# The first three rows of w4's last piece load ahead of the other w4 pieces, in transfers of 125 and of 3 partitions

## The chip, the core and the metric

The kernel runs on one core of a Trainium2 chip. A core has the engines PE (matrix multiply, with its weight loads PEld), DVE, ACT, POOL and SP, and sixteen DMA engines that move data between HBM and the on-chip memory SBUF, which has 128 partitions. Every load of this kernel but one is issued from SP. The metric is the device time of one execution in microseconds (us): the median of three runs is 218.01 (217.16 to 218.03).

## The reference

Two branches are computed for four tokens (B = 4, D = 576) and added to the input; all tensors are bf16.

- A: the token is normalized and multiplied by wq into 32 query heads of 128. Each pair of query heads attends to the last 2048 positions of one of 16 key/value heads; the result goes through wo (4096 x 576).
- B: an MLP. With one token per sequence its first shifted part adds zero, so that the branch is x plus gelu(layernorm(x) @ w3) @ w4, with w3 of 576 x 4608 and w4 of 4608 x 576.

```
xn = layernorm(x)
q = xn @ wq ;  p = softmax(q k^T * Dh^-0.5) ;  A = (p v) @ wo
h2 = gelu(layernorm(x1) @ w3) @ w4 ;  B = x1 + h2        # x1 = xn here
out = x + A + B
```

The keys and values that are read are 2 x 16 heads x 4 sequences x 2048 positions x 128 x 2 bytes, 67 MB; the weights bring the reads to 87.17 MB.

## The kernel before, in words

All large loads go through SP's queue in the order in which the program issues them. First come wq's five pieces and the 16 K tiles of 2 MB, one for each key/value head (`kv_load`, L98 to L102), with w3's five pieces between the first of them; then w4's first nine rows, then the 16 V tiles of 2 MB with the eight pieces of wo between them (L427 to L440), and last the remaining 27 row groups of w4.

A "row" of w4 in this text is one row group: `w4_src` (L106) views w4 as `[e, m, i, n]` with e = 2 halves, m = 128 partitions, i = 18 rows and n = 576 columns. One row holds 128 x 576 numbers, that is 1,152 bytes on each partition (144 KB). `load_w4(e, i0, n, cuts)` (L396 to L405) takes one buffer of the pool `w` (three buffers, used in turn) for n rows and issues one transfer for each entry of `cuts`. `mlp_out(t, e, i0, n)` (L407 to L409) multiplies: two matmuls of 288 columns for each row, which accumulate into the PSUM tile ACC (`acc_matmuls`, L328 to L331).

The end of the program is written out by hand:

```
    end = load_w4(0, 9, 9, (9,)) + load_w4(1, 0, 9, (9,)) + load_w4(1, 9, 9, (4, 2, 2, 1))   # L444
    run_later()
    mlp_out(*end[0])
    while later:
        run_later()
    for part in end[1:]:
        mlp_out(*part)
```

So six transfers follow the last V tile on SP: nine rows, nine rows, then the last piece of nine in cuts of four, two, two and one. PE takes them in the order of the list `end`: nine rows of the first, then what the list `later` still holds (the projection of the last head pair through wo, `project`, four rows of wo with two matmuls each), then nine, four, two, two and one rows. After the last matmul DVE copies ACC to the tile `fin` (L455), and SP and ACT each write half of the output with a transfer of 4 partitions (L457).

Each transfer from SP adds to one of eight semaphores, used in turn, and SP issues a transfer only after the transfer before it on the same semaphore has landed in full; so at most eight transfers are under way. A transfer of 128 partitions is shared by all sixteen DMA engines, each of which takes its share of every transfer in the order of issue and closes it with a 4-byte packet that adds one to the semaphore; the transfer has landed when the last engine has closed it.

Of the kernel before, what the change touches and what calls it, by code (L numbers as in the profile page):

```python
# [11 lines left out]
BF16 = mybir.dt.bfloat16  # L12
# [9 lines left out]
def kernel(  # L22
# [18 lines left out]
    nc = tc.nc  # L41
    P = 128
    B, Sq, D = A_x.shape
# [44 lines left out]
    wpl = ctx.enter_context(tc.tile_pool(name="w", bufs=NWP))  # L88
# [17 lines left out]
    w4_src = B_w4.rearrange("(e m i) n -> e m i n", e=2, i=NFH)  # L106
# [119 lines left out]
    for y in range(NY):  # L226
        tq = ps_o.tile([P, 2 * HB, P], BF16, tag="O", name=f"tq{y}")
        for k in range(2):
            for m in range(HB):
                nc.tensor.transpose(out=tq[:, k * HB + m, :],  # L230
                                    in_=q_rows[:, k, m, y, :, :].rearrange("p g i -> p (g i)"), identity=ident[:])
# [110 lines left out]
    def head_out(h):  # L342


        O, T = O_tiles.pop(h)
        on = small.tile([P, rep, B], BF16, tag="on")
        nc.vector.tensor_copy(out=on[:].rearrange("p r b -> p b r"), in_=O)  # L347

        def select():
            for x in range(XR):  # L350
                nc.tensor.matmul(out=T[0:32, x, :], lhsT=ident[:, x:P:XR], rhs=on[:].rearrange("p r b -> p (r b)"),  # L351
                                 start=(x == 0), stop=(x == XR - 1), skip_group_check=True)
            g2, odd = divmod(h, 2)
            if not odd:
                onx_tiles[g2] = small.tile([P, XR, B], BF16, tag="onx", name=f"onx{g2}")
            onx = onx_tiles[g2]
            for r in range(rep):
                q = 32 * (2 * odd + r)
                nc.vector.tensor_copy(out=onx[q:q + 32, :, :], in_=T[0:32, :, r * B:(r + 1) * B])  # L359
            if odd:  # L360
                wt = wo_tiles.pop(g2)
                onx_tiles.pop(g2)

                def project():
                    for x in range(XR):
                        acc_matmuls(onx[:, x, :], lambda a, z, x=x: wt[:, x, a:z])
                later.append(project)
        later.append(select)

    def run_later():  # L370
        fns = later[:]
        later.clear()
        for fn in fns:
            fn()
# [21 lines left out]
    def load_w4(e, i0, n, cuts):  # L396
        t = wpl.tile([P, n, D], BF16, tag="w", name=f"w4_{e}_{i0}")
        parts = []
        a = 0
        for m in cuts:  # L400
            nc.sync.dma_start(out=t[:, a:a + m, :], in_=w4_src[e, :, i0 + a:i0 + a + m, :])
            parts.append((t[:, a:a + m, :], e, i0 + a, m))
            a += m
        assert a == n
        return parts  # L405
# [29 lines left out]
    for v in range(Hkv):  # L435
# [5 lines left out]
        run_later()  # L441
        v_compute(v)
        head_out(v)
    end = load_w4(0, 9, 9, (9,)) + load_w4(1, 0, 9, (9,)) + load_w4(1, 9, 9, (4, 2, 2, 1))  # L444
    run_later()
    mlp_out(*end[0])
    while later:
# [40 lines left out]
```

## Time and profile before

| what | value |
|---|---|
| median of three runs | 218.01 us (217.16, 218.01, 218.03) |
| the profiled execution's own time | 217.48 us |
| its span | 215.6 us (1.9 us lie around it) |
| bytes read from HBM | 87.17 MB, 404 GB/s over the span |
| PE busy, DVE busy, ACT busy | 115.0, 108.9, 21.1 us |
| mean granted PE clock | 0.675 |
| share of the last chain: DMA, DVE, PE, ACT | 70%, 13%, 8%, 5% |

How to read it: times are in us from the span's start. The page's second part cuts the span into 40 equal slices of 5.39 us; a digit is a share in tenths. The windows view gives for chosen stretches the busy time of each engine, the granted PE clock (1.00 is full speed), the mean busy share of the sixteen DMA engines and the GB/s moved. The timeline lists instructions in order of time with start and duration. The trace also records every DMA packet (start, duration, bytes, queue, but not the DMA engine's number) and the moment of each addition to a semaphore.

### The profile page before, as it was taken

The numbers are of one execution on the slowest core, as the hardware profiler recorded it, in microseconds if no ns is written. First come the engines' busy times: TensorE is split into PE (matmuls) and PEld (weight loads), VectorE is DVE, ScalarE is ACT, GpSimd is POOL, SyncE is SP. The second block draws the span as 40 slices with busy tenths as digits, with TensorE's granted clock in tenths as the row PEclk, the third lists the DMA queues.
The fourth block names the chain that finished last, engine by engine and source line by source line (L and its number), as shares of the span: only waits on it lengthen the run. The fifth ranks groups of instructions, "written<-read, shape, count | busy, mean of one in ns | idle before, by whom it ended". The sixth has DMA issues, their size and how long they took to land.

```text
span 215.6 us, 5534 instructions
## 1 busy us (share of the span) xinstructions
PE 115.0 (53%) x2577; PEld 74.3 (34%) x2577; DVE 108.9 (51%) x156; ACT 21.1 (10%) x36; POOL 1.8 (1%) x8
## 2 busy tenths in 40 slices
PE   0343788748644554445424098748662634536383
PEld 0110744426311111111101087747452434434341
DVE  7932967584999999989785592201100000001000
ACT  0202220000000000000003896100000000000000
POOL 1110000000000000000000000000000000000000
PEclk9999999658767667558588557555555555555559
DMA  6999999999999999999999999999999999999970
GB/s 259 432 418 442 413 436 433 405 439 407 433 426 432 417 423 429 426 429 432 410 438 417 435 411 428 428 417 389 417 430 420 418 433 420 429 422 423 422 288 18
DMA packets 8255, 87.52 MB, mean 406 GB/s; under 512 B 925, under 2 KB 1065, under 8 KB 2729
## 3 DMA queue, kind: packets, MB, share of 16 engines
q1 hardware_dynamic: 8216, 87.17, 96.1%
q8 instruction: 20, 0.33, 0.6%
q14 instruction: 3, 0.02, 0.0%
q10 hardware_dynamic: 16, 0.01, 0.0%
HBM read 87.17 MB, written 0.00 MB: 404 GB/s over the span
## 4 chain that ended last, share of the span: by engine, by line
DMA 70%; DVE 13%; PE 8%; ACT 5%; issue 2%; SPq 1%; DVEq 0%; ACTq 0%
DMA t<-in_A_k_cache_dram 36%; DMA t<-in_A_v_cache_dram 21%; DMA w<-in_B_w_dram 9%; DVE kt L258 6%; DMA wq<-in_A_wq_dram 3%; PE pt L306 3%; PE O L325 2%; ACT E L283 2%; DVE qz L177 2%; PE qp L204 1%; ACT PZ L312 1%; ACT pr L300 1%; DVE mx L279 1%; DVE pr L302 1%; PE ACC L330 1%
## 5 line engine op out<-in xcount | busy, mean ns | idle before, releaser
L258 DVE STREAM_TRANSPOSE kt<-t 128x2048 int32<-128x2048 int32 x32 | 72.3, 2292 | 12.8 <-DMA t<-in_A_k_cache_dram 12.8
L267 PE MATMUL S<-kt,qz 32*32 32x512 bf16 x1024 | 36.9, 625 | 38.0 <-DVE kt L258 36.6
L325 PE MATMUL O<-PZ,t 128*128 128x8 bf16 x1024 | 30.3, 168 | 26.2 <-DMA t<-in_A_v_cache_dram 22.6
L325 PEld LDWEIGHTS <-t 128*128 128x128 bf16 x1024 | 29.0, 104 | 30.2 <-DMA t<-in_A_v_cache_dram 25.2
L347 DVE CAST on<-O 128x8 bf16<-128x8 f32 x16 | 2.7, 167 | 57.9 <-PE O L325 57.8
L267 PEld LDWEIGHTS <-qz 32*32 32x32 bf16 x1024 | 10.8, 94 | 60.6 <-issue 57.4
L306 PE MATMUL pt<-ident,pr 128*128 128x128 bf16 x64 | 6.7, 292 | 9.4 <-DVE pr L302 8.2
L383 PEld LDWEIGHTS <-w 128*128 128x128 bf16 x144 | 9.2, 162 | 5.2 <-DMA w<-in_B_w_dram 2.7
L383 PE MATMUL ACC<-ln2T,w 128*128 128x4 bf16 x144 | 9.6, 202 | 1.7 <-DMA w<-in_B_w_dram 1.7
L330 PE MATMUL ACC<-wo,onx 128*4 128x288 bf16 x64 | 9.0, 436 | 2.2 <-DVE onx L359 2.2
L283 ACT ACTIVATE E<-S,nb 128x512 f32<-128x512 f32 x4 | 4.0, 1115 | 59.5 <-DVE nb L281 59.5
L306 PEld LDWEIGHTS <-pr 128*128 128x128 bf16 x64 | 5.9, 135 | 10.0 <-ACT pr L300 10.0
L300 ACT ACTIVATE pr<-E,rdm 128x512 bf16<-128x512 f32 x6 | 8.1, 1430 | 0.8 <-DVE rdm L289 0.8
L359 DVE CAST onx<-O 32x16 bf16<-32x16 f32 x32 | 5.3, 165 | 5.3 <-PE O L351 4.9
L330 PE MATMUL ACC<-w,gT 128*4 128x288 bf16 x72 | 7.5, 368 | 0.8 <-DMA w<-in_B_w_dram 0.7
L302 DVE TENSOR_SCALAR pr<-E,rdm 128x512 bf16<-128x512 f32 x10 | 6.5, 809 | 0.3 <-PE pt L306 0.2
L204 PE MATMUL qp<-wq,xnT 128*4 128x512 bf16 x32 | 4.0, 620 | 4.5 <-DMA wq<-in_A_wq_dram 4.5
L224 DVE CAST q_rows<-qp 128x256 bf16<-128x256 f32 x8 | 2.9, 410 | 6.4 <-PE qp L204 6.4
L351 PE MATMUL O<-on,ident 128*32 128x8 bf16 x64 | 4.1, 171 | 3.6 <-DVE on L347 3.6
L351 PEld LDWEIGHTS <-ident 128*32 128x32 bf16 x64 | 4.4, 110 | 3.4 <-issue 3.1
L330 PEld LDWEIGHTS <-gT 128*4 128x4 bf16 x72 | 3.9, 104 | 4.7 <-issue 2.1
L330 PEld LDWEIGHTS <-onx 128*4 128x4 bf16 x64 | 3.7, 110 | 4.3 <-DVE onx L359 2.6
(67 smaller groups left out, 51.0 us busy)
## 6 DMA issues: line engine op xcount, KB each, us to landing
t<-in_A_k_cache_dram SPq DMA_DIRECT2D x16, 2048.0 KB, 24.7
t<-in_A_v_cache_dram SPq DMA_DIRECT2D x16, 2048.0 KB, 29.3
w<-in_B_w_dram SPq DMA_DIRECT2D x4, 1152.0 KB, 13.3
wo<-in_A_wo_dram SPq DMA_DIRECT2D x8, 576.0 KB, 21.3
wq<-in_A_wq_dram SPq DMA_DIRECT2D x4, 1024.0 KB, 6.3
w<-in_B_w_dram SPq DMA_DIRECT2D x3, 1296.0 KB, 30.3
w_t<-in_B_w_dram SPq DMA_DIRECT2D x1, 576.0 KB, 14.4
w<-in_B_w_dram SPq DMA_DIRECT2D x1, 576.0 KB, 25.1
```

What stands on the lines that cost most here:

```text
L204: nc.tensor.matmul(out=qp[k][32 * i:32 * i + B, :], lhsT=lhsT, rhs=rhs, start=False, stop=False, skip_group_check=True)
L258: nc.vector.transpose(out=ap32(kt, e * G * 2, [[2 * G * 2, NCH // 2], [1, 2], [2, G]]), in_=ap32(kn, e * G, [[2 * 2 * G, NCH // 2], [2 * G ...
L267: nc.tensor.matmul(out=S[g][32 * b:32 * b + 32, :].rearrange("p (c k l) -> p c k l", k=GK, l=2), lhsT=qz[32 * g:32 * g + 32, b, h, y, :], ...
L283: nc.scalar.activation(out=E[:, :, g, :].rearrange("p (c l) k -> p c k l", l=2), in_=S[g][:].rearrange("p (c k l) -> p c k l", k=GK, l=2), ...
L300: nc.scalar.mul(out=dst, in_=src, mul=rdm[:, b:b + 1])
L302: nc.vector.tensor_scalar_mul(out=dst, in0=src, scalar1=rdm[:, b:b + 1])
L306: nc.tensor.transpose(out=tp[:, cc, :], in_=pr[:, half * HC + cc, :, :, :].rearrange("p g k b -> p (g k b)"), identity=ident[:])
L325: nc.tensor.matmul(out=O, lhsT=vn[:, c, :], rhs=PZ[:, c, :].rearrange("p (b n) -> p b n", b=B)[:, :, h * rep:(h + 1) * rep], start=(c == 0 ...
L330: nc.tensor.matmul(out=ACC[32 * q:32 * q + B, 0:DH], lhsT=lhsT, rhs=rhs_cols(q * DH, (q + 1) * DH), start=False, stop=False, skip_group_ch ...
L351: nc.tensor.matmul(out=T[0:32, x, :], lhsT=ident[:, x:P:XR], rhs=on[:].rearrange("p r b -> p (r b)"), start=(x == 0), stop=(x == XR - 1), ...
L359: nc.vector.tensor_copy(out=onx[q:q + 32, :, :], in_=T[0:32, :, r * B:(r + 1) * B])
L383: nc.tensor.matmul(out=gp[:, fc, :], lhsT=lhsT, rhs=rhs, start=False, stop=False, skip_group_check=True)
```

## The change

Only the end changes. The tile of the last piece, `end_t`, is taken from the pool first. Its rows 0 to 2 are loaded right behind the last V tile, in one transfer of partitions 0 to 124 and one of partitions 125 to 127. Then come the two pieces of nine rows as before, and then the six remaining rows of the last piece in cuts of three, two and one. In PE's order the three rows stand behind the first nine rows and the projection, and ahead of the second nine. Seven transfers take the place of six; bytes, matmuls and what is computed stay the same.

```
-    end = load_w4(0, 9, 9, (9,)) + load_w4(1, 0, 9, (9,)) + load_w4(1, 9, 9, (4, 2, 2, 1))
+
+    end_t = wpl.tile([P, 9, D], BF16, tag="w", name="w4_end")
+    for p0, p1 in ((0, 125), (125, P)):
+        nc.sync.dma_start(out=end_t[p0:p1, 0:3, :], in_=w4_src[1, p0:p1, 9:12, :])
+    end = load_w4(0, 9, 9, (9,)) + [(end_t[:, 0:3, :], 1, 9, 3)] + load_w4(1, 0, 9, (9,))
+    for a, m in ((3, 3), (6, 2), (8, 1)):
+        nc.sync.dma_start(out=end_t[:, a:a + m, :], in_=w4_src[1, :, 9 + a:9 + a + m, :])
+        end.append((end_t[:, a:a + m, :], 1, 9 + a, m))
     run_later()
     mlp_out(*end[0])
     while later:
```

## The prediction

> **What bounds the kernel now.** I read the page's slices first, then the queues, then the chain of waits from 140 us on, then the windows of the last 10 us, and last PE's timeline there.
>
> ```profile
> PEclk9999999658767667558588557555555555555559
> DMA  6999999999999999999999999999999999999970
> GB/s 259 432 418 442 413 436 433 405 439 407 433 426 432 417 423 429 426 429 432 410 438 417 435 411 428 428 417 389 417 430 420 418 433 420 429 422 423 422 288 18
> ```
>
> The DMA engines are full in every slice from the second to the 38th. So the loads set the pace, and only the two ends of the span can be shortened without moving fewer bytes. The slice from 204.8 to 210.2 us moves 288 GB/s in place of some 422.
>
> ```profile
> 161.02 30.25 DMA t<-in_A_v_cache_dram
> ...
> 191.29 20.30 DMA w<-in_B_w_dram
> ...
> 211.63 0.68 PE ACC L330 x6
> ...
> 212.33 0.45 DVE fin L455
> ```
>
> The chain ends with the V tiles, w4's last transfers, six matmuls and the copy of ACC. After the copy stand the output's transfers, up to 215.6, which the change leaves alone.
>
> ```profile
> 204.00:206.00 2.00, 1.04 (x24) 0.83 (x23) 0.50 (x3) 0.00 (x0) 0.00 (x0) 0.50 1.00 417
> 206.00:208.00 2.00, 2.00 (x21) 1.07 (x17) 0.00 (x0) 0.00 (x0) 0.00 (x0) 0.50 0.88 344
> 208.00:209.00 1.00, 1.00 (x12) 0.53 (x10) 0.00 (x0) 0.00 (x0) 0.00 (x0) 0.50 0.53 209
> 209.00:210.00 1.00, 1.00 (x12) 0.57 (x10) 0.00 (x0) 0.00 (x0) 0.00 (x0) 0.50 0.42 150
> 210.00:211.00 1.00, 1.00 (x18) 0.64 (x16) 0.00 (x0) 0.00 (x0) 0.00 (x0) 0.83 0.26 83
> 211.00:212.00 1.00, 0.89 (x14) 0.41 (x9) 0.00 (x0) 0.00 (x0) 0.00 (x0) 1.00 0.07 23
> ```
>
> The last three columns are granted clock, DMA share and GB/s. The share falls in steps from 206 to 212: the sixteen engines do not finish together. Idle engine time there is 0.24 + 0.47 + 0.58 + 0.74 + 0.93 = 2.96 us for each engine on average; that is the most a perfect spread could take from the last landing. The additions to the semaphores say who is late: in the one-row transfer six engines close from 207.92 to 208.07, two at 208.26 and 208.85, four from 210.04 to 210.27, four from 211.46 to 211.96. The same groups stand in the last V tile (first 198.37, last 202.50).
>
> ```profile
> q1 hardware_dynamic: 8216, 87.17, 96.1%
> q8 instruction: 20, 0.33, 0.6%
> ...
> q10 hardware_dynamic: 16, 0.01, 0.0%
> ```
>
> Why they are late is in queue q8: 20 packets of 16 KB of instructions. Chaining the packet records (the next packet of an engine starts 3 or 4 ns before the last one ends) puts nearly all of them on eight engines in a fixed rotation, so that four have had three and four have had two; each costs its engine about 1.4 us. The other eight lead.
>
> The same windows show the second limit: PE is full from 206 to 211, at half clock until 210.33.
>
> ```profile
> 205.64 2.32 PE L330 MATMUL ACC<-w,gT 128*4 128x288 bf16 x18 [0.70 <-DMA w<-in_B_w_dram]
> 207.75 1.17 PE L330 MATMUL ACC<-wo,onx 128*4 128x288 bf16 x8
> 208.75 3.54 PE L330 MATMUL ACC<-w,gT 128*4 128x288 bf16 x36
> ```
>
> From the landing of the first nine rows (205.60) to the end PE works off 62 matmuls, 31 rows. Starts of successive rows lie 0.24 us apart at half clock and 0.12 at full clock. The second nine land at 208.70, just as PE is free; PE then waits only for the last two pieces (landed 211.58 and 211.96), about 0.3 us in all. So the last landing binds, but PE is only 0.4 us behind it.
>
> **The change, part by part.**
>
> *How the transfer is shared out.* Queue q1 counts 8216 packets: 57 transfers of 128 partitions with 128 + 16 closing packets make 8208, and one output transfer of 4 partitions with 4 + 4 makes the other 8; q10's 16 are two of 4 partitions. So 128 partitions run on 16 engines and 4 on four, evenly in both rows. The largest even split of 125 in at most 16 is five engines with 25 partitions each, of 3 on three. No transfer here shows 125: the bounds are one engine and sixteen. On one engine the 432 KB take 16.7 us at the price below, its first nine rows land at 201.5 + 16.7 = 218.2 and the end comes 12.6 us later, 230; I give that under 1 in 100. I take five, since both rows split evenly over as many as divide them. [...]
>
> *Price of the move.* A row of 3,456 bytes lies between those of 2,304 (eight take 0.735 us on an engine, 25.1 KB/us) and of 4,608 (1.40 us, 26.3 KB/us); I use 25.8. Each of the five gets 25 x 3.456 = 86.4 KB, 3.35 us, ahead of the second-to-last pieces, and three of them 0.13 more. In return every engine has 27.6 KB, 1.07 us, less behind the second nine. Net: eleven engines end 1.07 earlier, five end 2.28 later (2.41 with the small transfer).
>
> *One more transfer on SP.* An issue takes 0.33 us. The waits of SP for its eight semaphores come up once more; the last issue now waits for wo's last piece (landed 197.6) rather than V's tile before last (196.2), 8 us before any engine is through the last V tile and its w4 rows. Nothing queues behind it but the output. Price zero; if that lead were gone, the 1.4 us between the two landings. The tile takes an earlier buffer of the pool, last read by w3's matmuls, 140 us before; the two other tiles move to buffers freed in the softmax stage. Zero as well.
>
> *PE.* The three rows move ahead of the second nine; PE still has 31 rows to do after the first nine land, and that is what is late next. If the first nine still land at 205.60, PE does 4.69 us at half clock (until 210.33), 19.5 rows; the other 10.5 steps at 0.12 take 1.26, so the last row starts at 211.59 where now it starts at 212.00: gain 0.41. The last landing would be 211.96 - 1.07 = 210.89 and no longer binds. So of 1.07 us on the DMA side PE gives back 0.66.
>
> *The clock.* In the trace the granted clock changes only in steps that are multiples of 3.413 us, and it rose after one such step in which PE was full throughout. Where the grid lies against the kernel is not set by the program. The half clock could thus last 3.41 to 6.83 us from PE's start: last row at 205.64 + 3.6 + half of that, 210.95 to 212.65. Against the kernel before (the later of 212.00 and that) the gain is 1.05 us at most and nothing at least. [...]
>
> *Sum.* 217.48 - 0.41 = 217.07 on the profiled execution. That one lies 0.53 under the median of the runs, 218.01. I add half of that: **217.3 us**. This holds if the five engines are among the eight that lead.
>
> **The rivals.**
>
> *The five include late engines.* The trace has no engine numbers, so this is the open point. [...] If one of the latest is among them, its first nine rows land at 205.60 + 3.35 (+ 0.13) = 208.95 to 209.08 and PE starts 3.4 later. Its one-row piece lands at 211.96 + 2.41 = 214.37, and PE's last row starts at the later of that and 209.1 + 3.6 + 0.6 to 2.3 (step from 210.33 or 213.74), 214.4 to 215.0. That is 2.4 to 3.0 later, up to 4.1 with the worst grid: 219.9 to 221.6, most likely 220.4. It decides from the point where an engine is over 205.60 - 3.35 = 202.25 in the first nine. Nine of the sixteen are past that, one of them by 0.2 us only (it would cost the forecast 0.1 to 0.2); that speaks for it, the other seven against.
>
> *Only engines of the middle group.* They land the first nine at 203.68 to 203.89; plus 3.48 gives 207.37. PE starts 1.75 later and ends 0.5 to 2.2 later: 218.0 to 219.7.
>
> *The change does not do what it says: sixteen engines share the 125 partitions.* Then no load moves from one engine to another. The first nine land 1.07 later, at 206.67; PE starts at 206.71 and would start its last row at 206.71 + 3.6 + 1.8 = 212.1, with the last landing where it was: 0.1 slower, up to 0.85 with another grid; 217.6 to 218.4. Against it stand the two evenly split rows above. [...]
>
> *PE takes all of it.* Within the forecast: with the half clock at its longest, 6.83 us, PE ends at the same moment in both kernels, 0.0.
>
> **How the numbers follow.** Leading engines 46 in 100, late ones 36, middle ones 10, sixteen engines 8. The forecast's own range is 216.4 (the profiled run less 1.05) to 218.0. For 8 in 10 the range must reach into the late case: its likeliest 220.4 with 0.4 for the median gives 220.8. It starts at 216.3. About 0.5% (1.1 us) is what a measurement of this kernel can tell from no change. Faster by more than that is the forecast only with a good grid: 0.12. Same: 34 of the forecast's 46, all 8 of the sixteen, 3 of the middle: 0.45. Slower: 36 and 7, 0.43.
>
> **What would show each step.** Queue q1 should count 8208 packets: three end pieces of 144, one of 125 + 5 and one of 3 + 3 in place of four of 144, with 5 and 3 additions of the DMA engines to the two semaphores. In the last transfer the spread of the sixteen additions, now 4.04 us, should fall to about 3.0, with five of the leaders back by some 2.3 us. In PE's timeline the start on the first nine rows should stay at 205.6; in the rival it is 2 to 3.5 us later and PE's idle time before it grows from 0.70. The last wait of PE should go, and the granted clock should rise while PE is still busy. The prediction is wrong if the DMA share of 206 to 208 rises but the last landing is later than 212, or if one of the five is over 0.8 us behind the first engine in the last V tile.

## The result, and the profile after

The changed kernel takes 220.04 us (median of six runs, 219.12 to 220.56) against 217.83 for the kernel before (six runs, 217.16 to 218.03): a ratio of 1.0105, 95% interval 1.0078 to 1.0132. It is slower by 2.2 us, where 217.3 was forecast. The profiled execution took 220.56 us with a span of 218.8, against 217.48 and 215.6; it is the slowest of its six, so that differences read from its trace (3.1 us in all) are larger than the 2.2 us of the medians.

The page of the changed kernel, its slices of DMA and GB/s and its queues:

```profile
DMA  7999999999999999999999999999999999999970
GB/s 254 439 389 443 416 435 433 406 427 429 421 425 425 422 431 428 428 425 428 419 432 422 428 416 421 434 382 436 407 432 425 428 412 436 426 417 290 333 295 3
...
q1 hardware_dynamic: 8208, 87.17, 96.2%
q8 instruction: 20, 0.33, 0.6%
```

The DMA row still says 9 in slices 37 and 38 (197 to 208 us), and yet these move 290 and 333 GB/s in place of 423 and 422. The engines are not idle; their packets take longer. The windows view shows it apart from the slices, first the kernel before, then the changed one (the last three columns are granted clock, DMA share, GB/s):

```profile
198.00:200.00 2.00, 0.36 (x8) 0.28 (x5) 0.49 (x3) 0.00 (x0) 0.00 (x0) 0.50 1.01 426
200.00:202.00 2.00, 0.00 (x0) 0.00 (x0) 0.00 (x0) 0.00 (x0) 0.00 (x0) 0.50 0.98 407
202.00:204.00 2.00, 1.45 (x54) 1.45 (x55) 0.00 (x0) 0.00 (x0) 0.00 (x0) 0.50 1.00 425
```

```profile
198.00:200.00 2.00, 0.91 (x29) 0.84 (x25) 0.49 (x3) 0.00 (x0) 0.00 (x0) 0.50 1.08 283
200.00:202.00 2.00, 0.00 (x0) 0.00 (x0) 0.00 (x0) 0.00 (x0) 0.00 (x0) 0.50 1.02 255
202.00:204.00 2.00, 0.00 (x0) 0.00 (x0) 0.00 (x0) 0.00 (x0) 0.00 (x0) 0.50 0.99 237
```

A share of 1.0 with 237 to 283 GB/s is the sign to learn here: full engines at 60% of their rate. The packet records of the same stretch say who is slow: all. From 199 to 203 us the 3,456-byte packets of the new transfer take 228 ns on average (15 KB/us), the 16 KB packets of the last V tile 1,030 ns, the 10 KB packets of the next piece 651 ns; outside the stretch the same sizes take 138, 617 and 393 ns. The stretch lasts from 197.8 to 205, as long as packets of the 125-partition transfer are under way.

What that moves is in the chain of waits and in PE's timeline of the changed kernel:

```profile
185.54 23.43 DMA w<-in_B_w_dram
...
209.01 6.50 PE ACC L330 x62
```

```profile
209.01 2.32 PE L330 MATMUL ACC<-w,gT 128*4 128x288 bf16 x18 [0.75 <-DMA w<-in_B_w_dram]
...
212.08 0.93 PE L330 MATMUL ACC<-w_end,gT 128*4 128x288 bf16 x6
```

The first nine rows land at 208.97 (205.60 before), PE starts on them 3.37 us later, does its 62 matmuls without a gap and ends 3.2 us later. The last V tile, which stands ahead of the new transfer in every engine's queue, is late by the same amount: its last engine closes at 205.83 (202.50 before).

### The profile page after: what moved, and what is told of

The parts are those of the page before. It is cut to its first block, busy times and chain, and to the rows that moved or that the text cites. A ratio compares the mean times of both kernels' runs of the same rounds, so it can differ in the third digit from the quotient of the medians.

```text
span 218.8 us, 5535 instructions
## 1 busy us (share of the span) xinstructions
PE 114.8 (52%) x2577; PEld 74.2 (34%) x2577; DVE 108.9 (50%) x156; ACT 21.0 (10%) x36; POOL 1.8 (1%) x8
## 3 DMA queue, kind: packets, MB, share of 16 engines
q1 hardware_dynamic: 8208, 87.17, 96.2%
## 4 chain that ended last, share of the span: by engine, by line
DMA 64%; PE 14%; DVE 13%; ACT 5%; issue 2%; SPq 0%; DVEq 0%
DMA t<-in_A_v_cache_dram 26%; DMA t<-in_A_k_cache_dram 23%; DMA w<-in_B_w_dram 15%; DVE kt L258 6%; PE O L325 4%; PE ACC L330 4%; PE pt L306 3%; ACT E L283 2%; DVE qz L177 2%; ACT PZ L312 1%; PE qp L204 1%; ACT pr L300 1%; PE ACC L383 1%; DVE pr L302 1%; PE O L351 1%
## 5 line engine op out<-in xcount | busy, mean ns | idle before, releaser
L330 PE MATMUL ACC<-w,gT 128*4 128x288 bf16 x54 | 5.9, 389 | 0.7 <-DMA w<-in_B_w_dram 0.7
```

The costliest lines, as they stand in the source:

```text
L330: nc.tensor.matmul(out=ACC[32 * q:32 * q + B, 0:DH], lhsT=lhsT, rhs=rhs_cols(q * DH, (q + 1) * DH), start=False, stop=False, skip_group_ch ...
```

## The experiments

Theories of the slow stretch: **ports** (an engine writes at full rate only into its own partitions; a transfer that is not 128 wide sends engines into partitions that others fill), **few engines** (a transfer on fewer than sixteen engines slows the rest), **source** (five engines reading neighbouring rows of w4 collide in HBM). Beside them stands the rival of the prediction, that late engines were among the five. The traces do not name the engine of a packet. So which partitions are an engine's own was my assumption, and in the texts below "lowest" is only a name for the engines that a transfer of fewer than sixteen partitions runs on; an engine that writes outside its own partitions is called a stray. Each ratio is to the kernel before, run on the same chip.

**e1_wide128: the order alone.** From the changed kernel:

```
-    for p0, p1 in ((0, 125), (125, P)):
+    for p0, p1 in ((0, P),):
```

> The three rows go ahead of the other w4 pieces in one transfer of 128 partitions; all else as in the changed kernel. In the changed kernel's trace every DMA engine fell from some 26 KB/us to some 15 KB/us from 198 to 205 us, while five engines ran the rows of the 125-partition transfer. If the narrow sharing is the cause (all three theories on it below), no packet slows here: 3,456-byte rows at 25 KB/us, the first nine rows land about 1.07 us later than before, at 206.7, and the time is 0 to 0.9 us over the kernel before. If the order of the rows or the third-last position of the load were the cause (rival), the slow stretch and most of the 2.2 us stay.

Measured: 218.36 us, ratio 1.003 (1.0014 to 1.0047). Its windows:

```profile
198.00:200.00 2.00, 0.26 (x4) 0.17 (x3) 0.39 (x3) 0.00 (x0) 0.00 (x0) 0.50 1.05 438
200.00:202.00 2.00, 0.00 (x0) 0.00 (x0) 0.00 (x0) 0.00 (x0) 0.00 (x0) 0.50 0.95 392
202.00:204.00 2.00, 1.69 (x63) 1.69 (x64) 0.00 (x0) 0.00 (x0) 0.00 (x0) 0.50 1.02 429
```

No slow stretch is left: the 3,456-byte rows take 137 ns, and the first nine rows land at 206.44, 0.8 us later than before where the changed kernel is 3.4 us later. So 0.65 us of the 2.2 (by the ratio; 0.9 by the medians) belong to the order of the rows, and the rest to the way they are shared out.

**e2_96_32: sixteen engines, but not 128 partitions.**

```
-    for p0, p1 in ((0, 125), (125, P)):
+    for p0, p1 in ((0, 96), (96, P)):
```

> The same three rows in transfers of 96 and of 32 partitions: the even split over sixteen engines is 6 and 2 partitions each. Ports theory (an engine writes at full rate only into its own partitions, and a transfer that is not 128 wide sends engines into partitions that others fill): the 3,456-byte packets and those beside them slow to 13 to 16 KB/us for as long as these rows last, about 1.8 us in place of 1.07, time 0.5 to 1.5 us over e1_wide128. Few-engines theory (any transfer on fewer than sixteen engines slows the others): no slowing, the time of e1_wide128 within 0.3 us. Source theory (five engines that read neighbouring rows of w4 collide in HBM): no slowing.

Measured: 220.38 us, ratio 1.013 (1.0099 to 1.0161); 2.0 us over e1, more than expected.

Its queue q1 on the page, and its windows:

```profile
q1 hardware_dynamic: 8232, 87.17, 96.1%
```

```profile
198.00:200.00 2.00, 0.27 (x5) 0.21 (x4) 0.49 (x3) 0.00 (x0) 0.00 (x0) 0.50 0.94 247
200.00:202.00 2.00, 0.00 (x0) 0.00 (x0) 0.00 (x0) 0.00 (x0) 0.00 (x0) 0.50 0.93 347
202.00:204.00 2.00, 0.00 (x0) 0.00 (x0) 0.00 (x0) 0.00 (x0) 0.00 (x0) 0.50 1.01 285
```

8232 = 56 x 144 + 112 + 48 + 8: both transfers ran on sixteen engines, and the rate fell to 247 GB/s all the same, stood at 347 from 200 to 202, and fell again, to 285, from 202 to 204; I took the two dips for the leading and the late engines reaching the rows. A small number of engines is not needed for the loss: the few-engines theory falls, and so does the source theory, since five neighbouring readers are gone.

**e3_own5 and e4_foreign5: five partitions for each transfer, taken for the engines' own and for those of others.** To e1, ahead of its three rows, five transfers of 82 KB, 410 KB in all:

```
+    scr = kvp.tile([P, NCH, Dh], BF16, tag="kv", name="scr")
+    scr_f = scr[:].rearrange("p c d -> p (c d)")
+    src5 = v_win[0, 0:5].rearrange("h (p c) d -> h p (c d)", p=G)
+    for k, p0 in enumerate((0, 1, 2, 3, 32)):        # e4: (64, 65, 66, 67, 96)
+        nc.sync.dma_start(out=scr_f[p0:p0 + 17:4, :], in_=src5[:, k, :])
```

> As e1_wide128, and five extra transfers of 5 partitions (82 KB for each of five engines, rows of 16 KB of the V cache, into a scratch tile that nothing reads) ahead of the three rows. Partitions 0, 4, 8, 12, 16, then 1, 5, 9, 13, 17 and so on, and last 32, 36, 40, 44, 48. [...] Ports theory: the extra packets run at 26 KB/us and no other engine slows; five engines are 3.1 us later. Few-engines theory: about 15 KB/us on all sixteen for some 5 us. Source theory: 26 KB/us.

> [...] Source, rows, bytes and count of engines are the same. Ports theory: the extra packets run at about half rate (13 KB/us), the owners' packets too, and the others at least partly; a slow stretch of 5 to 7 us. Few-engines theory: the same as e3_own5, whatever that is. Source theory: 26 KB/us.

Measured, one run each: e3 217.11 us, e4 220.83 us. The windows of e3, then of e4:

```profile
198.00:200.00 2.00, 0.17 (x4) 0.08 (x3) 0.32 (x2) 0.00 (x0) 0.00 (x0) 0.50 0.98 390
200.00:202.00 2.00, 0.00 (x0) 0.00 (x0) 0.00 (x0) 0.00 (x0) 0.00 (x0) 0.50 0.95 385
```

```profile
198.00:200.00 2.00, 0.26 (x4) 0.17 (x3) 0.42 (x3) 0.00 (x0) 0.00 (x0) 0.50 1.14 254
200.00:202.00 2.00, 0.00 (x0) 0.00 (x0) 0.00 (x0) 0.00 (x0) 0.00 (x0) 0.50 1.00 209
```

Source, bytes, row length and width of the transfers are the same; only the partitions differ. In e3 the median 16 KB packet takes 613 ns as elsewhere, and 410 KB more cost nothing: the five engines had that much lead. In e4 packets take twice as long: 16 KB in 1,250 ns (median), 209 GB/s from 200 to 202 or 13 KB/us for an engine on average, and 190 to 254 GB/s over the six microseconds from 198 to 204. Of the three theories only ports fits this pair: the rate depends on the partitions written. Which engine wrote which of them is not shown, and neither is whether a stray slows the others by itself, or only while another engine writes into the same partitions.

**e5_own8: eight engines.** As e3, with eight partitions in place of five in each extra transfer (`scr_f[p0:p0 + 29:4, :]`).

> As e3_own5, with the extra transfers 8 partitions wide (partitions 0, 4, ... 28, then 1, 5, ... 29 and so on, last 32, 36, ... 60): 82 KB for each of eight engines, 655 KB in all, that nothing reads. Ports theory: no packet slows. If the eight engines that lead are the eight lowest, the late engines are not touched and the first nine rows land as in e1_wide128, about 206.4, time within 1 us of e1_wide128. If a late engine is among the eight, that landing comes some 3 us later and the time is about 221.

Measured: 220.63 us, one run. Its windows, and PE's start on the first nine rows:

```profile
198.00:200.00 2.00, 0.13 (x4) 0.04 (x2) 0.33 (x2) 0.00 (x0) 0.00 (x0) 0.50 0.99 404
200.00:202.00 2.00, 0.00 (x0) 0.00 (x0) 0.00 (x0) 0.00 (x0) 0.00 (x0) 0.50 0.99 405
```

```profile
209.29 2.32 PE L330 MATMUL ACC<-w,gT 128*4 128x288 bf16 x18 [4.80 <-DMA w<-in_B_w_dram]
```

No packet slows (404 to 411 GB/s from 198 to 204), yet the time is up. Of the eight engines, six close the first extra transfer from 198.06 to 199.05 and two at 202.60 and 202.63. So two of these eight are late; loaded with 3.1 us more they hold up the first nine rows until 209.24. This is the rival of the prediction as it had been described, here without any slow packet, and it shows that its trace looks different from that of the change: the last V tile is on time, and PE stands idle for 4.80 us before the first nine rows, where the changed kernel shows 0.75.

**e7_one_row: a third of the bytes.** In the changed kernel one row goes in 125 + 3 partitions, the other two behind it in one transfer of 128.

```
-        nc.sync.dma_start(out=end_t[p0:p1, 0:3, :], in_=w4_src[1, p0:p1, 9:12, :])
+        nc.sync.dma_start(out=end_t[p0:p1, 0:1, :], in_=w4_src[1, p0:p1, 9:10, :])
+    nc.sync.dma_start(out=end_t[:, 1:3, :], in_=w4_src[1, :, 10:12, :])
```

> The changed kernel with one row in place of three in the 125 and 3 partitions, the other two rows behind it in one transfer of 128. Ports theory: the slow stretch is about a third as long, 2 to 2.5 us in place of 7, and costs 0.8 to 1.0 us in place of some 2.8; first nine rows land at 207.0 to 207.6; time 218.8 to 219.4. If the slowing is a fixed cost of a narrow transfer, whatever its size: the time of the changed kernel, about 220.

Measured: 217.82 us, ratio 1.0031 (1.0017 to 1.0045). The slow stretch shrinks as expected, to 197 to 200 us (291 GB/s from 198 to 200), so the loss is no fixed cost of a narrow transfer. But the time is that of e1 (ratio 1.003), lower than I expected. In the profiled execution the first nine rows land 0.5 us later than in e1 (206.97 against 206.44), and the execution is only 0.2 us longer (217.61 against 217.38): here the granted clock rose 3.1 us after PE's start on them, in e1 3.9 us after.

**e8_foreign2: transfers of two partitions.** As e4 with two partitions (64 and 68, and so on) in place of five.

> [...] If a stray write holds up only the owner of the partition, the 16 KB packets beside it split in two groups: the two strays and the two owners at about half rate (1.2 us), the other twelve engines at 0.61 us. If it holds up all sixteen, as the even durations in e4_foreign5 suggest, all 16 KB packets lengthen together, by as much as the strays' or by less.

Measured: 220.84 us, one run; the windows of e8:

```profile
198.00:200.00 2.00, 0.25 (x4) 0.16 (x3) 0.32 (x2) 0.00 (x0) 0.00 (x0) 0.50 1.08 219
200.00:202.00 2.00, 0.00 (x0) 0.00 (x0) 0.00 (x0) 0.00 (x0) 0.00 (x0) 0.50 1.02 214
```

Between 198 and 201 the 16 KB packets take 1,258 to 1,304 ns, with no second group at 613. Transfers two partitions wide slow the packets beside them as far as transfers five wide do. As far as two and five tell, the loss depends on how long such a transfer is under way, not on whether it is two or five wide.

**e6_lead8 and e9_lead4: useful bytes meant for leading engines, in partitions taken for their own.** In e6 rows 14 to 17 of w4's last piece are laid out over partitions 0 to 63 alone, in eight transfers of 8 partitions, in e9 rows 16 and 17 over partitions 0 to 15 and 32 to 47, in eight transfers of 4, all on ACT's queue. The matmuls that make the gelu input are cut to match: 20 more in e6, 70 more in e9. The loads of e9:

```
+            for hi in range(2):
+                for j in range(4):
+                    p0 = 32 * hi + j
+                    nc.scalar.dma_start(out=sp[p0:p0 + 13:4, :, :, :], in_=w4s[1, hi, j, :, :, NFH - NS:NFH, :])
...
-    end = load_w4(0, 9, 9, (9,)) + load_w4(1, 0, 9, (9,)) + load_w4(1, 9, 9, (4, 2, 2, 1))
+    end = load_w4(0, 9, 9, (9,)) + load_w4(1, 0, 9, (9,)) + load_w4(1, 9, 7, (3, 2, 1, 1))
```

> [...] Behind the last V tile come nine, nine, two, two and one rows, all 128 wide. Ports theory, with the eight lowest engines leading: every late engine has four rows, 1.4 us, less at the end, PE has 27 rows in place of 31 after the first nine land; the last row starts 0.5 to 1.0 us earlier than before: 216.5 to 217.2, ratio 0.995 to 0.998. If the eight are not the leaders, or if eight small transfers cost more than they move: 218 to 221.

> [...] Behind the last V tile come nine, nine, three, two, one and one rows, 128 wide. Late engines have two rows, 0.74 us, less at the end, PE two rows less after the first nine land; no packet slows. Last landing 0.7 us and last matmul 0.3 to 0.6 us earlier than before, unless the 140 more instructions of PE put one more instruction packet (about 1.4 us) on a late engine: 216.6 to 217.3, ratio 0.996 to 1.000.

Measured: e6 218.35 us, ratio 1.0039 (1.0019 to 1.006), as its second branch said. That e5 found two late engines among the eight of its transfers is a reason for it that was not tested further. e9 215.36 us, ratio 0.9905 (0.9882 to 0.9928): faster than both kernels, and by more than I expected. Three runs take that apart.

**e10_lead4_again, e11_extra_mm, e12_lead16.** e10 is e9 again. e11 adds 80 small matmuls and eight gelu columns, cut like e9's, to the kernel before and moves nothing. e12 is e9 with the two rows loaded by two transfers of 16 partitions:

```
-                for j in range(4):
-                    p0 = 32 * hi + j
-                    nc.scalar.dma_start(out=sp[p0:p0 + 13:4, :, :, :], in_=w4s[1, hi, j, :, :, NFH - NS:NFH, :])
+                nc.scalar.dma_start(out=sp[32 * hi:32 * hi + 16, :, :, :], in_=w4s[1, hi, :, :, NFH - NS:NFH, :])
```

> The kernel of e9_lead4, unchanged, again. Its gain (2.07 us, ratio 0.9905) was larger than the two rows can explain (0.74 us on the late engines), and its 16 KB packets took 611 to 613 ns in stages where all others show 616 to 618, its instruction packets 932 ns in place of some 1,065. If the gain belongs to the kernel: ratio 0.988 to 0.993 again. If it was the placement of that one run: ratio 0.996 to 1.000, with packets and instruction packets as elsewhere.

> The kernel before with the 80 small matmuls on w3 and eight gelu columns of e9_lead4 added, their result unused, and no row moved: w4's last piece is loaded 128 wide in four, two, two and one as before. If moving the rows is what gains: the time of the kernel before or up to 0.5 us over it, ratio 1.000 to 1.003. If the longer PE program (other places of the instruction packets in time) is what gains: ratio 0.990 to 0.995.

> e9_lead4 with its 16 + 16 partitions of rows 16 and 17 loaded in two transfers of 16 partitions, shared by all sixteen engines, one partition each. [...] Ports theory: 295 KB squeeze through four engines' partitions, for about 2.8 us at least; the packets beside them slow while these run, near 150 to 160 us, and the time is 1 to 3 us over e9_lead4: 216.5 to 218.5. If only the layout and the earlier multiplication of the two rows gained: the time of e9_lead4.

Measured: e10 215.03 us, ratio 0.9889 (0.987 to 0.9908); e11 216.15, ratio 0.9942 (0.9929 to 0.9955); e12 218.05, ratio 1.003 (1.0013 to 1.0047). The gain repeats. More than half of it, 1.3 of 2.4 us, comes with e11's additions even when nothing is moved, as the second branch of its expectation said; the other 1.1 us (216.15 less 215.03) is what the moved rows can account for at most, since e10's packets are a little shorter than e11's as well. And e12, with the same layout and the same data in the same places, loses 3.0 us to e10 when it moves these 295 KB in transfers of 16 partitions in place of 4 (the "four engines' partitions" of its expectation are the places that e9's transfers of 4 fill; that they belong to four engines was my assumption). The windows of e10, then of e12, where these loads run (the ACT queue issues e12's at 116.1 and 120.7, so earlier than I expected):

```profile
120.00:125.00 5.00, 2.31 (x22) 2.18 (x23) 4.65 (x10) 4.14 (x4) 0.00 (x0) 0.50 1.01 431
125.00:130.00 5.00, 4.25 (x93) 3.82 (x90) 4.00 (x7) 4.23 (x5) 0.00 (x0) 0.84 0.99 413
```

```profile
120.00:125.00 5.00, 2.39 (x23) 2.26 (x24) 4.63 (x10) 4.21 (x4) 0.00 (x0) 0.50 1.02 340
125.00:130.00 5.00, 4.17 (x92) 3.74 (x90) 4.06 (x7) 4.54 (x5) 0.00 (x0) 0.84 1.01 319
```

Full engines again, at 340 and 319 GB/s in place of 431 and 413: (91 + 94) x 5 us at 425 GB/s is 2.2 of the 3.0 us.

## Why the prediction was wrong

It was wrong in the direction and by 2.7 us: a gain of 0.7 on the median was forecast, and 2.2 were lost. Step by step:

- **What bounds the kernel: right.** The last landings set the end, with PE close behind. In the changed kernel PE's start on the first nine rows again carries all of the difference. The groups of six, two, four and four engines hold for the one-row transfer; in the last V tile they are six, two, five and three, which changes no sum.
- **Five engines, three engines: right.** Queue q1 counts the 8208 packets that were named, and the semaphores show 5 and 3 additions by DMA engines. e3 and e5 count 8266 and 8296, which is 5 + 5 and 8 + 8 packets for each extra transfer.
- **That the five lead: right, and the condition of the forecast was met.** In the changed kernel's last V tile five engines close from 198.28 to 198.35, ahead of all others, and all five run rows of the new transfer from about 198 on. The chances of 46, 36 and 10 in 100 for leading, late and middle engines were my estimate; no run shows how the five are chosen among the sixteen. So the late-engine rival, whose 220.4 is near the 220.04 measured, did not happen. Its number was right for a reason that was not there, and the range reached up to 220.8 for this rival alone, so that the measured time lies in it is luck. One of the prediction's own signs tells the two apart: PE's start on the first nine rows moved by 3.4 us, as in the rival, but its idle time before it stayed at 0.75 (0.70 before), because the last V tile was late too. In e5, where the rival happened, it is 4.80. The prediction's own sign of being wrong came as well: the DMA share of 206 to 208 us rose, from 0.88 to 0.99, and the last landing came at 214.24.
- **The price of the move: this step failed.** The prediction priced a 3,456-byte row of the narrow transfer at 25.8 KB/us, between two rows of 128-partition transfers, and let every other engine run on as before. The narrow transfer ran at 15 KB/us (5.5 to 7.3 us for the five engines, not 3.35), and the other eleven fell to about the same rate (16 KB packets at 15.9 KB/us), the last V tile included, which was not even behind it. At 255 in place of 425 GB/s, 7 us lose 2.8 us. So eleven engines did not end 1.07 us earlier, and the first nine rows did not land at 205.60 but at 208.97. The bound from both sides did not hold it either: one engine or sixteen were both priced at the full rate. The rows that the price came from were all of transfers of 128 partitions, and the trace of before had no large row of another width.
- **PE: right.** PE did 31 rows with no gap. With the clock rising 5.19 us after PE's start, at 214.20, the formula gives a last start of 209.01 + 3.6 + 2.6 = 215.21, as measured. The changed kernel's clock records, too, hold only stretches of whole multiples of 3.413 us (3.413 to 81.92, but for the last, which ends with the trace), and their place moved: the rise at 128.41 us before is at 128.87 after, while PE's matmuls at 143.26 start at the same time in both.
- **One more transfer on SP: right.** Its issues came 8 us or more ahead of need.
- **Sixteen engines, the third rival:** e1 is that case, 128 wide. Its 0.65 us by the ratio lie within the 0.1 to 0.85 worked out, its 0.9 by the medians just above. The 0.85 was too low as a bound: by the prediction's own formula, 206.71 + 3.6 + 3.4 = 213.7, PE can end up to 1.7 later where a clock step falls between the two starts. e2 is sixteen engines with other widths, and there the price failed as it did for five.

What the runs showed in place of the failed step: the rate depends on which partitions a transfer goes to, and how wide it is.

| run | partitions of its narrow transfers | 16 KB packets beside them | GB/s |
|---|---|---|---|
| e3 | five at a time, in 0 to 19 and 32, 36, ... 48 | 613 ns (median) | 385 to 396 from 198 to 204 |
| e5 | eight at a time, in 0 to 31 and 32, 36, ... 60 | not slowed | 404 to 411 from 198 to 204 |
| e10 | four at a time, in 0 to 15 and 32 to 47 | - | 413 to 432 from 115 to 140 |
| e12 | sixteen at a time, 0 to 15 and 32 to 47 | - | 340 and 319 from 120 to 130 |
| e4 | five at a time, in 64 to 83 and 96, 100, ... 112 | 1,250 ns (median) | 190 to 254 from 198 to 204 |
| e8 | two at a time, 64 and 68, 65 and 69 and so on | 1,258 to 1,304 ns | 219 and 214 from 198 to 202 |

That each engine has partitions of its own fits these runs, but no trace shows which engine wrote which, here or in the 125 partitions. Why such a transfer holds up the packets of all sixteen engines was not settled; the even durations in e8 say only that it does.

## What to carry to other kernels

Cut to 125 and 3 partitions, or to 96 and 32, a load slowed every transfer beside it here, to some 255 GB/s in place of 425 in the first case. So before a load is cut to another number of partitions, run the cut alone, and count as its price the slowing of every transfer that runs beside it, for as long as it runs. A DMA share of 1.0 with fewer GB/s than elsewhere in the same kernel, and longer packets of the same size, are the sign of it. To even out engines that finish at different times, lay the data out so that the leading engines have more, in partitions where a run shows no slowing (e9, which gains at most 1.1 us by it), and check from the closings of a transfer which engines lead, since here six of the eight in e5 did and two did not.

## What the runs showed of the hardware that was not expected

- Transfers of two partitions cost as much as those of five: 16 KB packets at 1,258 to 1,304 ns (e8) and at about 1,250 ns (e4), with no second group at 613 ns in e8.
- The slowest rows of the change, four at 300 to 482 ns from 203.5 to 204.3 us, stand by their order between the closing packets in the 125-partition transfer, on its last two engines; the three rows of the 3-partition transfer, between closings at 202.9 and 203.2, took 207 to 221 ns. Why the four took longest stays open.
- Additions that move no byte made the kernel faster: e11, with 80 more matmuls and eight more gelu columns, has a ratio of 0.9942. Its 16 KB packets take 612.2 ns on average from 170 to 196 us where the kernel before has 616.5, and those of e9, e10 and e12 611.0; but e6, which also has more matmuls, shows 616.2. From 40 to 196 us the averages are 615.1 in e11 and 617.4 before; on 156 us of full engines that is an estimated 0.6 us of e11's 1.3. In e9 and e10 the instruction packets take some 933 ns (975 in e12), in all others 1,056 to 1,076, e11 among them. The trace does not say why; this stays open.
